# Packed attention, gate and gated MLP on one core: weight folds over four row blocks at once, raw weights in later places, one flat order

## The chip, the core and the metric

The kernel runs on one core of a Trainium2 chip. The time is device microseconds of that core for one execution. Before the change the median of three runs is 605.56 us (605.19 to 606.15).

## The reference, cut to what matters

```
def sm_attn(qq, kk, vv):                                  # float32, scale = 1/8
    s = scale * qq @ kk^T; s = s - max(s)
    a = exp(s); a = a / (sum(a) + 1e-9)
    return a @ vv
p_packed = sm_attn(p, k, v)                               # p: 8 batches, 8 heads, 32 packed queries, 64
x = sm_attn(q, p_packed, p_packed)                        # q, k, v: 8, 8, 576, 64 -> x: 8, 576, 512
gate = sigmoid(causal depthwise convolution of x, 5 taps) # conv_w 5, 512
x = (gate * (x @ w_val)) @ w_out                          # both 512, 512
h = relu(x @ w_in); u, v = h[..., :512], h[..., 512:]     # w_in 512, 1024
v_n = (v - mean(v)) / sqrt(var(v) + 1e-6)
v_s = w_spatial @ v_n + b_spatial                         # over the 576 positions
out = (u * v_s) @ w_out2                                  # 512, 512
```

The weights of the two later parts arrive as float64 words. The kernel makes float32 of them on the chip.

## The kernel before, in words

**Layout.** Channels lie on the 128 partitions, in four blocks, and the 576 positions on the free axis. Large products are made in three passes of split numbers: a value is cut into a high part, which ScalarE casts, and a remainder, which VectorE subtracts (`split`, L134 to 137), and `mm3` (L143) multiplies high by high, high by remainder and remainder by high. All of PSUM is one pool, `ps2`, of four tiles of two banks each.

**Weights.** A raw block is 128 rows of 512 float64 words. `load_raw` (L553) loads it, and `from_f64` (L536 to 547) turns it into float32: ScalarE reads both halves of each word in two passes (L539, L544), VectorE shifts and adds (L545, L547). One such conversion is a unit. Since nothing stands between the gated values and `w_in` but the product with `w_out`, the kernel multiplies these two weights once, in `fold` (L571 to 582), and keeps the product, split, in `wp`. `fold(m, hf)` makes row block m of one half of the columns: four matmuls of 128x512 over k = 0 to 3, in one PSUM tile, then the high part on ScalarE (L580) and the remainder on VectorE (L582). The half of `w_in` that gives v is `winv` (`fv`, hf = 1), the other `winu` (`fu`, hf = 0). The raw blocks lie two by two in the places of later tiles: `w_out` in `wo20` and `ws1`, the v half in `wo21` and `vn1`, `w_val` in `wo20` and `wo21` after those, the u half in `ws1` and `wo20`; the converted u half goes into `wo21`. `spatial` (L584) loads and splits `w_spatial`, `final` (L605) does so with `w_out2`.

**Attention of one batch.** `sa` (L186) makes the scores of the packed queries against k in two PSUM tiles, their maximum and exponential; `tr` transposes; `av` (L228) multiplies by v and divides by the sum, which ends p_packed (`pp`); `ppt` (L258) transposes it. `sb` (L265) makes the scores of q, also in two PSUM tiles, `sn` (L277) their softmax up to the exponential, `sb2` (L292) the sum, the division and a transpose, and then the split into `Ah` and `Al`. `m` (L310) multiplies p_packed by `w_val` to `Mh` and `Ml` (M in what follows), so that `val` (L386) needs only A times M. `xt` (L326) makes x itself, `cv` (L364) the convolution of one channel block in one ScalarE step and four VectorE taps, and the gate from it. For the first batch `cx` makes the gate on TensorE instead, in two halves of 80 matmuls, with tap weights that `cw`, `cb` and a part of `av` prepare.

**MLP of one batch.** `val` makes gate times value, split, for one channel block. `hv` makes one of five position blocks of v, its relu and its normalisation; `hu` one channel block of u; `sp` the spatial product times u, split; `out` one block of the output, which it stores. All of `val`, `hv`, `hu`, `sp` and `out` issue their matmuls at L141.

**What sets the order.** Each piece is a generator, and `run` (L691) walks a written order: a token such as `0hv2.3` takes the generator `hv(2)` of batch 0 three steps further. Tokens without a batch digit are setup pieces or the attention of the first batch; with the digit b, a piece of the attention belongs to batch b + 1. Every engine gets its instructions in just this order and waits in it. SP issues all loads and stores, in order as well. HEAD holds the setup and batches 0 to 2, STEP one batch of the middle (used three times), LAST the end. Loads are tokens too: `ro`, `rw`, `rv` and `ru` raw blocks, `ik`, `ip`, `iv` and `ic` the first k, p, v and conv_w, and `lk`, `lv`, `lp` and `lq` the later ones (k and q share three places, v has two). The name `fv1` repeated four times is thus one fold, step by step.

Of the kernel before, what the change touches and what calls it, by code (L numbers as in the profile page):

```python
# [25 lines left out]
m0 0uu2 cx0 fv0 0uu2 m0.2 0uu2 fv0 cx0 0val2.2 0uu1 0val3 0val2 0val0 0uu1 0val2 0val3 0val2 0val0 0uu1 0val3 0val1
0val0 0val3 0sa0 0val0 0val3 0uu3 0lq0.2 0val1 0val0 1lp0.2 0lq1.2 0uu3 0val1 0uu3 0fu3.3 0sa0 0val1 0fu0 0wo0 0fu3
0fu0 0fu3 0fu0 0fu3 0sa0 0fu0 0val1 0hv0 0wo0 0fu0 0tr0.2 0wo1 0sa0 0wo0 0fu0 0hv4 0tr1.2 0hv0.2 0hv1 0hv4 0hv0 0wo1
0hv4 0hv0 0hv4 0wo1 0hv0 0av0 0hv4 0wo3 0wo1 0hv2 0lv0.2 0av0 0hv4 0hv0 0av0 0wo1 0hv4 0hv1 0hv4 0hv1 0fu2 0wo3 0hv4.2
0fu2 0hv1 0wo3 0hv2 0fu2.2 0hv2 0lk0.2 0wo3 0hv3 0fu2 0hv1 0hv2 0wo3 0fu2 0hv1 0hv2 0hv1 0hv2 0av1 0hv2 0hv3 0fu1 0hv3  # L30
0lv1.2 0fu1 0av1 0hv3 0av1 0fu1 0hv3.2 0ppt0 0fu1 0hv3 0ppt0 0m0 0ws4 0wo1 0fu1 0wo3 0ws4 0sb0.2 0ws0 0fu1 0ws3 0ws0
0hu0 0m0 0lk1.2 0sn1 0wo2 0wo0 0ws4 0hu0 0ws1 0m0 0sn1 0hu1 0hu0 0ws4.2 0sb21 0hu1 0ws2 0wo2 0hu2 0hu1 0ws2 0sb21
0ws4.2 0hu3 0wo2 0hu3 0ws1 1lq0.2 0wo2 0sb21 0hu2 0hu3 0wo2 0ws3 0sp3 0hu2 0wo0 0sn0 0sp2 0wo2 0sn0 0sp2 0sb20 0sp1
0sp2 0sb20 0sp1 0sp2 0sb20 0sp2 0sp0 0sp1.3 0sp0 0xt0 0sp0 0sp3 0sp0 0xt0.2 0sp0 0xt1 0sp3.2 0xt1.2 0sp3 0out3 0cv1
0out2 0cv2 0cv1 0cv0 0out2 0cv3 0out0 0out2 0cv3 0cv1 0out2 1val1 0out0 0cv2 0cv3 1val3 0out0 1val1 0out0 1val3 0out3
# [15 lines left out]
3lq1.2 3val3 3hv0 4lp0.2 3lk1.2 3sa0 3hv1 3hv0.2 3sa0 3hv3 3hv0.2 3hv1 3tr0.2 3sa0 3hv1 3hv2 3hv0 3tr1.2 3hv1 3hv0
3hv1 3hv3 3hv1 3hv3 3av1 3av0 3hv1 3hv3 3lv0.2 3av1 3hu1 3hv2 3lv1.2 3av0 3av1 3hv2 3av0 3hv4 3hv3 3hv2 3hv3 3hv2 3hv3
3hv2 3hu1 3hv4 3hv2 3hv4 3hu2 3hv4 3hu1 3hv4 3hu3 3hv4.3 3ppt0 3hu3 3ppt0 3hv4.2 3sb0.2 3hu3 3sp1 3sn1 3lk0.2 4lq0.2
3sp3 3sn0 3sn1 3sp1 3sb21 3sn0 3hu0 3hu2 3sp1 3sb21 3sb20 3hu0 3hu2 3sp1 3sp2 3hu0 3sp1 3sb20 3sb21 3sp0 3sb20 3sp0
# [723 lines left out]
```

## Time and profile before

| what | value |
|---|---|
| median of three runs | 605.56 us |
| the profiled execution | 605.75 us, its span 603.9 us |
| TensorE busy | 575.3 us, 5267 matmuls |
| VectorE busy | 448.3 us |
| ScalarE busy | 300.3 us |
| DMA, mean over the span | 87 GB/s, 52.55 MB |

The page's second part cuts the span into 40 slices of 15 us. Each digit is the busy share of a slice in tenths (9 is 90% or more); the line DMA is the mean share of the 16 DMA engines:

```profile
PE   1499999999999999999999999999999999999997
DVE  3677879689668988588687987698778978597330
DMA  8990344013220252013220232012311200020002
```

The span is the time from the first to the last instruction that the profiler saw; the measured time also holds 1.85 us around it. A busy time counts only instructions that compute, and the ends of matmuls are modelled. The mean over the span hides that the start and the end look unlike the middle.

### The profile page before, as it was taken

The page shows a single profiled execution, that of the slowest core. Times are in us where ns is not written, and L with a number is a line of the kernel's source. Part 1 is how long each engine was busy: PE and PEld are TensorE (multiplying, and loading weights), DVE is VectorE, ACT ScalarE, POOL GpSimd, SP SyncE. Part 2 cuts the span into 40 slices and gives each one's busy share as a digit, 9 for nine tenths or more (in the row PEclk, how much of TensorE's full clock was granted, in tenths as well). Part 3 has the DMA queues.
Part 4 walks back from the last instruction along what each step waited for, and adds up shares of the span by engine and source line. Part 5 has one row for each costly group of instructions (what it writes and reads, how often), then busy time and mean ns, then how long its engine had stood idle before and what let it go on. Part 6 is the DMA issues. An engine that isn't in the chain of part 4 may idle for free.

```text
span 603.9 us, 12467 instructions
## 1 busy us (share of the span) xinstructions
PE 575.3 (95%) x5267; PEld 504.7 (84%) x5267; DVE 448.3 (74%) x847; ACT 300.3 (50%) x524; POOL 31.2 (5%) x51
## 2 busy tenths in 40 slices
PE   1499999999999999999999999999999999999997
...
DVE  3677879689668988588687987698778978597330
...
DMA  8990344013220252013220232012311200020002
...
DMA packets 16615, 52.55 MB, mean 87 GB/s; under 512 B 1968, under 2 KB 2992, under 8 KB 16560
## 3 DMA queue, kind: packets, MB, share of 16 engines
...
q14 instruction: 14, 0.11, 0.1%
...
## 4 chain that ended last, share of the span: by engine, by line
PE 82%; DVE 9%; DMA 5%; ACT 3%; issue 1%; SPq 0%; DVEq 0%
PE ps L141 71%; PE ps L577 4%; DVE acc L371 4%; DMA kq<-qT 2%; DMA raw<-w_in 2%; PE ps L269 2%; PE ps L234 2%; PE ps L191 1%; DVE g L137 1%; PE ps L332 1%; DMA raw<-w_outT 1%; DVE g L501 1%; PE ps L316 1%; ACT g L135 1%; ACT x L340 1%
## 5 line engine op out<-in xcount | busy, mean ns | idle before, releaser
L141 PEld LDWEIGHTS ps<-ws,vn 128*128 128x128 f32 (+1 forms) x896 | 119.6, 188 | 3.6 <-ACT u L480 1.9
L141 PE MATMUL ps<-ws,vn 128*128 128x288 f32 (+1 forms) x896 | 122.3, 296 | 0.0
L141 PE MATMUL ps<-g,wo 128*128 128x288 f32 x768 | 107.1, 296 | 1.4 <-ACT g L135 0.8
L141 PE MATMUL ps<-g,wp 128*128 128x288 f32 x768 | 107.7, 297 | 0.0
L141 PEld LDWEIGHTS ps<-g,wo 128*128 128x128 f32 x768 | 103.1, 188 | 4.9 <-ACT x L340 2.2
L141 PEld LDWEIGHTS ps<-g,wp 128*128 128x128 f32 x768 | 104.3, 188 | 2.6 <-DVE wp L582 0.5
L371 DVE SCALAR_TENSOR_TENSOR acc<-x,cw,acc 128x572 f32<-128x572 f32 (+1 forms) x112 | 90.1, 815 | 7.6 <-ACT acc L367 4.6
L141 PE MATMUL ps<-wp,g 128*128 128x512 f32 x384 | 94.0, 400 | 1.0 <-DVE g L137 1.0
L141 PEld LDWEIGHTS ps<-wp,g 128*128 128x128 f32 x384 | 71.0, 188 | 20.3 <-issue 2.1
L135 ACT CAST g<-g 128x576 fp32r<-128x576 f32 x64 | 42.8, 674 | 71.4 <-DVE g L501 53.0
L137 DVE TENSOR_TENSOR g<-g,g 128x576 fp32r<-128x576 f32 x64 | 48.2, 753 | 22.9 <-ACT g L135 22.2
L448 POOL TENSOR_TENSOR rstd<-rstd,mhalf 128x1 f32<-128x1 f32 (+1 forms) x40 | 27.3, 683 | 514.0 <-DVE rstd L446 506.6
L501 DVE TENSOR_TENSOR g<-ps,u 128x576 f32<-128x576 f32 x32 | 23.9, 748 | 31.8 <-PE ps L141 31.8
L141 PE MATMUL ps<-Ah,Mh 128*128 128x288 f32 x128 | 38.1, 298 | 0.5 <-DVE Ml L137 0.4
L135 ACT CAST vn<-vr 128x512 fp32r<-128x512 f32 (+1 forms) x40 | 25.1, 627 | 26.2 <-DVE vr L450 26.2
L141 PE MATMUL ps<-Ah,Ml 128*128 128x288 f32 x128 | 37.8, 295 | 0.0
L141 PE MATMUL ps<-Al,Mh 128*128 128x288 f32 x128 | 37.8, 295 | 0.0
L442 DVE BATCH_NORM_STATS2 st<-vr 128x6 f32<-128x512 f32 (+1 forms) x40 | 27.5, 686 | 11.7 <-ACT vr L430 7.0
L430 ACT ACTIVATE vr<-ps 128x512 f32<-128x512 f32 x32 | 19.3, 602 | 32.7 <-PE ps L141 22.9
L137 DVE TENSOR_TENSOR vn<-vr,vn 128x512 fp32r<-128x512 f32 (+1 forms) x40 | 27.3, 682 | 7.8 <-ACT vn L135 7.3
L450 DVE TENSOR_SCALAR vr<-vr,mv,rstd 128x512 f32<-128x512 f32 (+1 forms) x40 | 21.7, 541 | 14.2 <-POOL rstd L448 14.0
L377 ACT ACTIVATE gate<-acc 128x576 f32<-128x576 f32 x28 | 19.2, 687 | 25.7 <-DVE acc L371 25.6
...
## 6 DMA issues: line engine op xcount, KB each, us to landing
...
```

The lines of the kernel that those rows point to most:

```text
L135: nc.scalar.copy(out=hi, in_=src)
L137: nc.vector.tensor_tensor(out=lo, in0=src, in1=f32(hi), op=ALU.subtract)
L141: nc.tensor.matmul(out, lhsT=a, rhs=b, start=(i == 0), stop=(i == len(pairs) - 1))
L234: nc.tensor.matmul(ps[NPK * h:NPK * h + NPK, :65], lhsT=aT[:, 9 * (h // 2) + 4 * (h % 2) + t, :], rhs=v[:, h, t, :], start=(t == 0), stop= ...
L371: nc.vector.scalar_tensor_tensor(out=acc[:, sft:], in0=x[:, :S - sft], scalar=cw[:, c, tap:tap + 1], in1=acc[:, sft:], op0=ALU.mult, op1=A ...
L377: nc.scalar.activation(out=gt, in_=acc, func=AF.Sigmoid)
L430: nc.scalar.activation(out=vr, in_=ps, func=AF.Relu)
L442: nc.vector.bn_stats(st[:w], vr[:w])
L448: nc.gpsimd.tensor_tensor(out=rstd[:w], in0=rstd[:w], in1=mhalf[:w], op=ALU.pow)
L450: nc.vector.tensor_scalar(out=vr[:w], in0=vr[:w], scalar1=mv[:w, 0:1], scalar2=rstd[:w], op0=ALU.subtract, op1=ALU.mult,)
L501: nc.vector.tensor_tensor(out=halves(t), in0=ps[:, :, :SH], in1=halves(self.u.pop(c)), op=ALU.mult)
L577: nc.tensor.matmul(ps, lhsT=woT[k][:, cs], rhs=win[k], start=(k == 0), stop=(k == NC - 1))
```

## The change: what it does

One order, `ORDER`, now writes out all eight batches, and `run` takes no first batch. All its pieces stand in a new order.

The folds no longer take four k in a row for one m. Two row blocks share a PSUM tile (`fps`), four are open at once, and the order takes one k for all m when that block of both weights is converted. Both halves together hold four PSUM tiles, which is all of them.

The raw blocks get places of their own: `w_out` where `wp0` comes to lie, the v half where `wp1` does, `w_val` in `Ml`, `Mh` and `wo20`, the u half in `ws1` and `wo21`. The converted u block is written over the first half of its own raw block. `wp` is therefore made only when the first fold has all its passes. Blocks are loaded one by one, and all four kinds use the early temporaries (pool `g`).

`sa`, `sn` and `sb2` have more places where they can stop, so that the order can put other pieces between their steps. `GATE0` is true, so the first gate is made as before. No instruction is added or left out on any engine.

```diff
--- before.py
+++ after.py
-HEAD = """
-cb0 ro0.2 ik0.2 ip0.2 ro1 ik1.2 lk0.2 ro1 ic0.2 uo0 iv1.2 uo0 uo1 iv0.2 uo1 uo0 rw1 uo1 rw1 uo2 rv0 uo2 sa0 rv0 uo2
-sa0 0ws4 uo3 rw0 cw0 rw0 cw0 0ws0 sa0 uo3 cw0 sa0 cb0 lq0.2 tr0.2 uo3 cb0 uw2 tr1.2 cb0 lq1.2 uw2 uw3 0ws1 uw3 uw2 uv0
-0ru0 uv0 uv1 uw3 lp0.2 av1 0lp0.2 cb0 uv1 uv0 uw0 av0 lv0.2 av1 uv1 av0 av1 uw1 av1 0ru1 av0 0ru1 ppt0 av0 uw0 ppt0
...
-STEP = """
-1val0.2 0out1 0out3 0out1 1val0 0out1 0cv1 0cv3 0out3 1val1 0out3 0out2 0out3 0cv2 0cv3 0out2 1val0 0out2 1val0 0cv2
...
+GATE0 = True
+ORDER = """
+ik0 ip0 ik1 ic0 cw0.3 cb0 rw0 uw0 sa0 cb0 ro0 sa0 cb0 uw0 uo0.2 rw1 uw1 iv1 cb0 sa0 uw0 uo0 fv3 fv2 sa0 uw1.2 ro1
+uo1.3 fv0 ru0 fv1 fv2 iv0 cb0 sa0 tr0 av0 tr1 av1 uu0 rw2 av0 lq0 uu0 uw2 av0 av1 uw2 fv1 av1 ppt0 fv3 uw2 lq1 ppt0
+ro2 uu0 ru1 rw3 av0 sb0 fv0 av1 sn1 uo2 lp0 uo2 fu0 sn1 uo2 uu1 sn0 rv2 uu1 sn1 uw3 ro3 sn1 uw3 uu1 sn0 fu1 uw3 ru3
+sn0 fv3 uo3.2 uv2 uu3 ru2 fv1 uv2 sb21 fu2 fv0 uo3 uu2 rv0 uu3 fv2 fu1 sn0 sb21 wo0 sb20 fu3.2 fu2 lk1 rv3 uu3 fv0 uv2
+uv0 uu2 fv2 uu2 sb21 fv1 sb21 sb20 fv1 sb20.2 rv1 fv1 uv1.2 fv3.2 fv0.2 sb21 uv3 fv3 fu0.2 fu3 fu2 fv2.2 fu3.2 fu0 fu3
+wo3 uv1 ws0 fu2 uv3 uv0 sb20 uv3 fu2.2 cx1 uv0 ws3 wo0.2 0lp0 0lq1 sb20 cx1 sb21 fu1 wo0 fu1.2 ws4 m0.2 wo3 m0 cx0 wo3
+0val0 wo3 fu1 ws3 lv1 ws1 cx0 fu0.2 0val0 ws3 ws2.2 ws4 0val3.2 0val1.2 0val0.2 0val3 0val2.2 0val0 ws1 0val1.2
+0val2.2 lk0 0val1 0val3 0val2 0sa0 0val3 0hv0.2 0sa0 0hv0.2 0sa0 0hv1 ws4 wo0 0hv1.2 0hv0 0sa0 0hu0 0tr0 0hv0.2 ws1
+0sa0 0tr1 0hv1 0hv2.2 0hv1.2 0hv2.2 wo3 0hu0 lv0 wo1 0av0.2 wo0 2lp0 0av0 0hv2 0av1.2 wo3 ws2 0hv4 ws0 0hv2.2 wo1 0hv1
+wo1 wo2 0hv3 0hu0 0hv4 0hv3 0av1 0hv4 0hu2 0hv3.2 0hv4.2 0ppt0 0hv4 0ppt0 ws0 0hu2.2 0lq0 0sb0 0sn1 0hv3.2 wo1 0hv4
+0hv3 0hu3.2 0sn0.2 0hu1.2 ws4.3 wo1 0sn0 0hv4.2 0sn0 ws4 0sn1.2 0sb20.2 0hv4 0sn1 0sb20.3 0sp2 0sp1.2 wo2 0hu3 0sb21.3
...
+0sp3.3 0xt1 0cv3 1val0.2 0sp3 0cv1 wo1 0sp3 0lk0 0out2 1val1.2 0out2 0cv0 0cv2 0out2 0cv1 0cv2 0out0 0out2 0out0.2
+0out1 0cv2 0cv0 0out1.2 0cv3 1val2.2 0out3 0cv1 1val1 0out3 0cv0 1val3 1val2 0cv3 1val3 1val2 1val0.3 1val3 1val1.2
+0out1 0lk1 0out3 1val2 1val3 1sa0 1val3 1hv2.2 1sa0.3 1tr0 1hv1.2 1hu3.2 1lq1 1hv0 1sa0 1hv1 1tr1 1hv2 1av1 1hv1 1av1
...
+6sp1.2 6m0 6sp1 6sn1 6sb21.2 6sp1 6sb21.2 6sp0.2 6sp2 6sb20 6xt0.2 6sp2 6sb21 6sb20 6sp0 6sb21 6sp0 5out2 6sp0 6xt1.2
+6cv1 6sp2 6sp1 6cv1 6sp3 6sp2 6sp3.3 7val2 6sp2 6cv2 6sp3 6cv0 7val0.2 7val2 6cv3 6out1.4 6cv1 6cv2.2 6out3.3 7val1.2
+6out2 6cv0.2 7val0 6out2 7val2 7val1 6cv3 6out0.2 7val0.2 7val1 6cv3 7val2 7val1 7val3.3 6out0 7val2 7val3.2 7hv3
+6out0 7hv3.4 7hv0 7hv3.2 7hv0.2 7hv1.4 7hv4 7hv1.3 7hv0 7hv4 7hu3.2 7hv4.7 7hv0 7hv2 7hu2 7hu3 7hv0 7hv4 7hv2 7hu2.2
+7hu1 7hv2 7hu1.2 7hv2.3 7hu0.3 7hv2 7hv0 7sp0.2 7sp2.2 7sp1 7sp2 7sp3 7sp0.3 7sp2.2 6out2 7sp1.2 7sp3.2 7sp1.2 7sp3.2
+6out2 6out3 7out1 7out0.3 7out2 7out1.3 7out3.4 7out0 7out2.3
 """
@@ -120,8 +124,7 @@
     ps2 = ctx.enter_context(tc.tile_pool(name="ps2", bufs=4, space=bass.MemoryType.PSUM))
 
     wval = const.tile([P, NC, DM], F32)
-    wp = [const.tile([P, NC, 2 * DM], F32R, name=f"wp{i}") for i in range(2)]
-    wo2, ws = [], []
+    wp, wo2, ws = [], [], []
     cw = const.tile([P, NC, CONV], F32)
     ident = const.tile([P, P], F32)
 
@@ -203,6 +206,7 @@
             m4 = sm_p.tile([NPK, 4, 8], F32, tag="m4", name="m4")
...
                 nc.vector.tensor_copy(m4[:, qt, :], mx[NPK * qt:NPK * qt + NPK])
+            yield
             m1 = sm_p.tile([NPK, 8], F32, tag="m1", name="m1")
...
...
-            if self.b == 0:
+            if self.b == 0 and GATE0:
...
@@ -280,8 +284,10 @@
             sTf = sT.rearrange("p a b -> p (a b)")
             for n in range(2):
                 nc.vector.transpose(out=sTf[:, n * SH:(n + 1) * SH], in_=ps[:, n, :SH])
+            yield
             mx = sm_p.tile([P, NB], F32, tag="mx2", name="mx2")
             nc.vector.tensor_reduce(mx, sT, axis=AX.X, op=ALU.max)
+            yield
             nc.vector.tensor_tensor(
                 out=sT, in0=sT, in1=mx.unsqueeze(2).to_broadcast([P, NB, NPK]), op=ALU.subtract
             )
@@ -293,11 +299,14 @@
             sT = self.sT.pop(g)
             sm = sm_p.tile([P, NB], F32, tag="sm2", name="sm2")
             nc.vector.tensor_reduce(sm, sT, axis=AX.X, op=ALU.add)
+            yield
             nc.vector.tensor_scalar_add(sm, sm, 1e-9)
             nc.vector.reciprocal(sm, sm)
+            yield
             nc.vector.tensor_tensor(
                 out=sT, in0=sT, in1=sm.unsqueeze(2).to_broadcast([P, NB, NPK]), op=ALU.mult
             )
+            yield
             an = an_p.tile([P, S], F32, tag="an", name="an")
             nc.vector.transpose(out=an, in_=sT.rearrange("p a b -> p (a b)"))
             self.an[g] = an
@@ -546,36 +555,55 @@
         yield
         nc.vector.tensor_tensor(out=dst, in0=dst, in1=t, op=ALU.add)
 
-    woT, winv, winu = [], [], []
     raws = {}
     early, late = (g_p, "g"), (cv_p, "cv")
-
-    def load_raw(name, slot, w, lo):
-        k0 = int(name[-1]) * 2
-        raw = (vn_p if slot == "vn1" else const).tile([P, 2, 512, 2], I32, tag=slot, name="raw")
-        for i in range(2):
-            if i:
-                yield
-            nc.sync.dma_start(out=raw[:, i], in_=words(w[:, k0 + i, lo:lo + DM]))
-            raws[name[:-1], k0 + i] = raw[:, i]
-
-    def unit(kind, k, dst, temps):
-        return from_f64(dst, raws.pop((kind, k)), DM, *temps)
-
-    def u_half(k):
-        if not winu:
-            t = const.tile([P, NC, DM], F32, tag="wo21", name="winu")
-            winu[:] = [t[:, k, :] for k in range(NC)]
-        return winu[k]
+    blocks = {}
+
+    def block(tag, k, n):
+        if tag not in blocks:
+            blocks[tag] = const.tile([P, n, 2 * DM], I32, tag=tag, name="raw")
+        return blocks[tag][:, k % n]
+
+    def one(tag):
+        return am_p.tile([P, 2 * DM], I32, tag=tag, name="raw", bufs=1)
+
+    places = {
+        "o": lambda k: block("wp0", k, NC),
+        "w": lambda k: block("wp1", k, NC),
+        "v": lambda k: block("wo20", k, 2) if k > 1 else one("Mh" if k else "Ml"),
+        "u": lambda k: block("wo21" if k > 1 else "ws1", k, 2),
+    }
+    homes = {
+        "o": lambda k: woT[:, k],
+        "w": lambda k: winv[:, k],
+        "v": lambda k: wval[:, k],
+        "u": lambda k: raws["u", k].bitcast(F32)[:, :DM],
+    }
+
+    def load_raw(kind, k, w, lo):
+        raw = raws[kind, k] = places[kind](k)
+        nc.sync.dma_start(out=raw.rearrange("p (n t) -> p n t", t=2), in_=words(w[:, k, lo:lo + DM]))
+        yield
+
+    def unit(kind, k):
+        raw = raws[kind, k].rearrange("p (n t) -> p n t", t=2)
+        return from_f64(lambda: homes[kind](k), raw, DM, *early)
+
+    fps = {}
 
     def fold(m, hf):
-        ps = ps2.tile([P, 2, 512], F32, tag="ps2", name="ps2")[:, 0, :]
-        win = winv if hf else winu
+        if (hf, m // 2) not in fps:
+            fps[hf, m // 2] = ps2.tile([P, 2, 512], F32, tag="ps2", name="ps2")
+        ps = fps[hf, m // 2][:, m % 2]
         cs = slice(P * m, P * m + P)
         hs = slice(hf * DM, (hf + 1) * DM)
         for k in range(NC):
-            nc.tensor.matmul(ps, lhsT=woT[k][:, cs], rhs=win[k], start=(k == 0), stop=(k == NC - 1))
-            yield
+            nc.tensor.matmul(
+                ps, lhsT=woT[:, k, cs], rhs=homes["uw"[hf]](k), start=(k == 0), stop=(k == NC - 1)
+            )
+            yield
+        if not wp:
+            wp[:] = [const.tile([P, NC, 2 * DM], F32R, tag=f"wp{i}", name=f"wp{i}") for i in range(2)]
         hi, lo = wp[0][:, m, hs], wp[1][:, m, hs]
         nc.scalar.copy(out=hi, in_=ps)
         yield
@@ -654,14 +682,14 @@
     setup = {
         "cw": lambda i: from_f64(lambda: cw.rearrange("p a b -> p (a b)"), cw64, NC * CONV, *early),
         "cb": lambda i: tap_rows(),
-        "ro": lambda i: load_raw(f"o{i}", ("wo20", "ws1")[i], w_outT, 0),
-        "rw": lambda i: load_raw(f"w{i}", ("wo21", "vn1")[i], w_in, DM),
-        "rv": lambda i: load_raw(f"v{i}", ("wo20", "wo21")[i], w_val, 0),
-        "ru": lambda i: load_raw(f"u{i}", ("ws1", "wo20")[i], w_in, 0),
-        "uo": lambda k: unit("o", k, lambda: woT[k], early),
-        "uw": lambda k: unit("w", k, lambda: winv[k], early),
-        "uv": lambda k: unit("v", k, lambda: wval[:, k, :], early),
-        "uu": lambda k: unit("u", k, lambda: u_half(k), late),
+        "ro": lambda k: load_raw("o", k, w_outT, 0),
+        "rw": lambda k: load_raw("w", k, w_in, DM),
+        "rv": lambda k: load_raw("v", k, w_val, 0),
+        "ru": lambda k: load_raw("u", k, w_in, 0),
+        "uo": lambda k: unit("o", k),
+        "uw": lambda k: unit("w", k),
+        "uv": lambda k: unit("v", k),
+        "uu": lambda k: unit("u", k),
         "fv": lambda m: fold(m, 1),
         "fu": lambda m: fold(m, 0),
         "ws": spatial,
@@ -688,11 +716,11 @@
             return getattr(mls[b], name)(i)
         return getattr(ats[b + 1], name)(i) if b + 1 < B else ()
 
-    def run(order, first):
+    def run(order):
         for tok in order.split():
             tok, _, n = tok.partition(".")
             name = tok.lstrip("01234567")
-            b = -1 if len(name) == len(tok) else first + int(tok[0])
+            b = -1 if len(name) == len(tok) else int(tok[0])
             key = b, name
             if key not in live:
                 live[key] = iter(steps(b, name[:-1], int(name[-1])))
@@ -701,15 +729,10 @@
 
     make_identity(nc, ident)
     nc.vector.memset(mhalf, -0.5)
-    t = const.tile([P, NC, DM], F32, tag="ws0", name="woT")
-    woT[:] = [t[:, k, :] for k in range(NC)]
-    t = vn_p.tile([P, NC, DM], F32, tag="vn0", name="winv")
-    winv[:] = [t[:, k, :] for k in range(NC)]
+    woT = const.tile([P, NC, DM], F32, tag="ws0", name="woT")
+    winv = vn_p.tile([P, NC, DM], F32, tag="vn0", name="winv")
     with tc.manual_schedule():
-        run(HEAD, 0)
-        for b in range(3, 6):
-            run(STEP, b)
-        run(LAST, 6)
+        run(ORDER)
```

## Rows read from the trace of the kernel before

**Rows 1.** The page, part 1: busy us (share of the span) and instructions.
```profile
PE 575.3 (95%) x5267; PEld 504.7 (84%) x5267; DVE 448.3 (74%) x847; ACT 300.3 (50%) x524; POOL 31.2 (5%) x51
```

**Rows 2.** Stretches of the start: busy us (instructions) of each engine, clock, DMA share, GB/s.
```profile
0.00:10.00 10.00, 1.22 (x32) 0.74 (x32) 2.12 (x6) 4.41 (x7) 2.08 (x8) 1.00 0.80 289
10.00:20.00 10.00, 3.18 (x40) 2.39 (x41) 7.04 (x20) 5.99 (x17) 0.00 (x0) 1.00 1.02 416
20.00:30.00 10.00, 4.79 (x94) 3.14 (x92) 6.63 (x16) 6.93 (x14) 1.76 (x3) 1.00 1.03 404
30.00:40.00 10.00, 8.94 (x43) 3.58 (x40) 7.29 (x14) 2.52 (x4) 0.00 (x0) 1.00 1.03 410
```

**Rows 3.** Stretches again, the fold's instructions (L577) alone.
```profile
8.00:55.00 47.00, 14.87 (x32) 6.04 (x32) 1.00 0.79 314
55.00:92.00 37.00, 14.44 (x32) 5.86 (x32) 1.00 0.35 115
```

**Rows 4.** Timeline of TensorE: start us, us, line, operation, count, idle before.
```profile
8.17 1.22 PE L191 MATMUL ps<-kq,pbd 64*32 64x144 f32 x32 [8.17 <-DMA pbd<-pT]
...
32.30 1.03 PE L577 MATMUL ps<-winv,woT 128*128 128x512 f32 x1
...
35.52 9.71 PE L577 MATMUL ps<-winv,woT 128*128 128x512 f32 x22 [0.90 <-DVE winv L547]
...
46.02 2.68 PE L351 MATMUL ps<-an,ppk 32*64 32x288 f32 x80
...
54.65 0.40 PE L141 MATMUL ps<-Ah,Mh 128*128 128x288 f32 x1 [0.42 <-DVE Ml L137]
...
60.41 1.27 PE L191 MATMUL ps<-kq,pbd 64*32 64x144 f32 x64
...
76.94 0.78 PE L234 MATMUL ps<-v,aT 128*32 128x65 f32 x40
...
91.33 1.09 PE L316 MATMUL ps<-wval,ppT 64*32 64x512 f32 x16
92.21 1.18 PE L269 MATMUL ps<-kq,ppT 64*32 64x288 f32 x32
```

**Rows 5.** Timeline of ScalarE: the conversion that waited for w_out's last block.
```profile
13.61 0.66 ACT L539 ACTIVATE tmp<-raw 128x512 f32<-128x512 f32 x1 [3.08 <-DMA raw<-w_outT]
```

**Rows 6.** Groups by line and form: count, busy us, mean ns, idle before.
```profile
L282 DVE STREAM_TRANSPOSE sT<-ps 128x288 f32<-128x288 f32 x32 | 13.5, 460 | 11.6 <-PE ps L269 11.6
...
L284 DVE TENSOR_REDUCE mx<-sT 128x18 f32<-128x576 f32 x16 | 12.0, 753 | 0.5
...
L137 DVE TENSOR_TENSOR Ml<-ps,Mh 128x1024 fp32r<-128x1024 f32 x8 | 9.8, 1223 | 2.3 <-ACT Mh L135 2.3
...
L135 ACT CAST Mh<-ps 128x1024 fp32r<-128x1024 f32 x8 | 8.2, 1028 | 1.4 <-PE ps L316 1.4
...
L582 DVE TENSOR_TENSOR wp<-ps,wp 128x512 fp32r<-128x512 f32 x8 | 5.5, 681 | 0.5 <-ACT wp L580 0.4
...
L210 DVE TENSOR_SCALAR nb<-m 32x8 f32<-32x8 f32 x32 | 5.2, 161 | 0.6
...
L547 DVE CUSTOM_DVE_ANT_0 woT<-woT,tmp 128x1024 uint16<-128x1024 uint16 x4 | 2.6, 678 | 0.1
...
L545 DVE TENSOR_SCALAR woT<-tmp 128x512 int32<-128x512 int32 x4 | 1.7, 425 | 7.1 <-ACT tmp L539 7.1
```

**Rows 7.** Timeline of the tail, VectorE's taps and TensorE.
```profile
534.21 6.65 DVE L371 SCALAR_TENSOR_TENSOR acc<-x,cw,acc 128x572 f32<-128x572 f32 x8
...
545.60 10.29 PE L141 MATMUL ps<-wp,g 128*128 128x512 f32 x43 [0.98 <-DVE g L137]
...
587.62 0.40 PE L141 MATMUL ps<-g,wo 128*128 128x288 f32 x1 [0.84 <-ACT g L135]
...
588.42 11.68 PE L141 MATMUL ps<-g,wo 128*128 128x288 f32 x86 [0.40 <-DVE g L137]
```

More of the change, by code (lines that the diff above doesn't have):

```diff
@@ L26 @@
[L26 to L35, printed above, removed]
@@ L51 @@
[L51 to L54, printed above, removed]
-3sp2 3sp0.3 3sp3 3sp2.2 3xt0 3sp2 3m0 3sp3 3xt0.2 3xt1 3sp3 3m0 3sp3 3out0 3xt1.2 3m0 3out0 3cv0 3cv1 3cv0 3out1 3cv2
@@ new lines @@
+1sn0 1sb20 1sn1.3 1sb21.3 0out0 1sb21 1hu2 1sb20.2 1sp3.2 1lv0 1sb21.2 1sp3.2 1sp2 1sp0.2 1sp3 1sb20.2 1sp1.3 1sb20
+1xt0.2 1sp1 1lk1 1sp2 0out3 1sp2.2 1sp0 1xt1.2 1cv0 2val0 1sp1 2val0 1cv3 1sp2 1out2.2 1cv0 1out2.2 1cv2 1cv3 1lv1
+1out0 1out1.2 1cv0 1cv1 1out3 1out0 1cv3 1out1 1out3.2 1cv1 2val0 2val1.2 2val2 1cv2 1cv1 2val1 1lp0 2val2 2val0.2
+2val3.2 1cv2 2val2 2val1 1lk0 2val1 1out0.2 2sa0 2val3 2val2.2 2val3 2lq1 2val3 2hv0 2hv3 2hv0 2sa0.2 2hu1.2 2sa0
+2hv0.2 2tr0 2sa0 2tr1 2hv3 2hu1 2hv0.2 2hv3 2hv0 2hu0 2hv2 2hv3.2 2av1.2 2hv3 2av0 2hv3 2hv2.3 2av1 2lv1 2av0.2 2hv1
@@ new lines @@
+2ppt0 2hv1.2 2ppt0 2hv1 2hu0 2sb0 2hv2 2sn0 2hv4 2hv2.2 2sn1 2hv4.3 2sn0 2hv1.2 2sn1 2hv4.3 2hu0 2hu2.2 2hv4 2sn1 2hv1
+2hu2 2hu3.3 2hv4.2 2sp1.2 2sn0.2 2sp1 2sb20 1out1 2sp0.2 2sb20 2sp1 2lv0 2sb20.2 2sp1 2sn1 2sb21.2 2sp2.2 1out3
+2sb21.3 2lk1 2sp0.3 2sb20.2 2sp2.2 2lk0 2sp3.3 2sp2 2xt0.2 2sp3.2 2m0.2 2xt1 2sb21 2xt1 2cv0 2m0 2out1 2cv3 2out1 2cv0
+2out1 3val2 2cv2 2cv3 2out2 2out0 2cv1 2out2 3val0.2 2out1 2out2.2 2cv1 3val1 2cv2 2cv0 3val0 3lq1 2out0.2 3val2 2cv3
+3val1 2cv1 3val1 2out3 2cv2 2out3 3val2 3val3.2 3val0.2 3val1 3sa0 3val3 3val1 3val2.2 3val3 2out3 3lq0 3val3 3hv0.2
```

57 lines of the change are left out of this document (25 added, 32 removed).

## The prediction

> **What bounds the kernel now.** I read the engine shares first, then the first 40 us slice by slice, then the order of TensorE's work there, and the tail last. TensorE is busy 575.3 of 603.9 us [rows 1], so 28.6 us are idle. The slices show where: busy 1.22, 3.18, 4.79 and 8.94 us of each 10 [rows 2] leaves 21.9 us idle before 40 us. In the tail an idle 0.98, 0.84 and 0.40 us stand in front of three runs of matmuls, and the last run ends at 588.42 + 11.68 = 600.1 [rows 7], 3.8 us before the end. That leaves 0.7 us for all batches between. Only the start can give much.
>
> In the start the transfers run flat out: DMA share 1.02 and 1.03 at 404 to 416 GB/s [rows 2]. TensorE has little to do because the fold (w_out times w_in) needs converted blocks of two weights, and a row block takes its four k in turn: its first pass is at 32.30, the long run at 35.52 [rows 4]. The V half's 32 passes stand ahead of 55 us, the U half's 32 behind it [rows 3], in time in which TensorE does nothing but work. The first matmul of `val` is at 54.65 [rows 4].
>
> **The change part by part.** Every engine issues the same instructions; no transfer is added. Order, places and waits change.
>
> *Transfers.* A raw block is 128 x 512 float64, 512 KB, 1.28 us at 410 GB/s. In the old order the eighth transfer (the last of four w_out blocks, three k and p: 3840 KB, 3.93 MB) was there at 13.6 [rows 5]; 3.93 MB are 9.6 us, so a landing is 4.0 us plus the bytes up to it. New order: both k and p, 1216 KB, at 7.0; the first pair (w_in's V block 0, w_out's block 0), 2260 KB with conv_w's 20, at 9.6; q, 6760 KB with both v (650 each), at 20.9; the last w_val block, 13032 KB, at 36.5. Each raw block lies in a place that nothing used before, so SP waits for none of the 16. It does wait at `0lq1`, until ScalarE has converted w_out2's block 0, with four loads and `lk0` behind it; `0sa0`, the next that needs them, comes some 10 us later, so I cost it at nothing; uncovered it would be some 4 us.
>
> *First fold.* Scores at 7.0 + 1.22 [rows 4] = 8.2. VectorE then has two 576-wide passes of 0.75, nine small of 0.16, two shifts of 0.42 and two adds of 0.68 [rows 6]: 5.1 us, with hops 13.7. From there TensorE folds k = 0 for all four m: four blocks, eight passes.
>
> *Clock.* The granted column prints 1.00 from the start [rows 2], but 32 score matmuls took 1.22 us at 8.17 and 64 took 1.27 us at 60.41 [rows 4]: at the start the array ran at its half level, 1.2 GHz. One fold pass still took 1.03 us at 32.30; 22 passes from 35.52 took 9.71, 0.43 each, at 2.4 GHz [rows 4]. It rose in between, when scores and folds had run almost without pause. So in the new order a pass costs 0.86 or 0.43. I take four of the first eight at the half level: 5.2 us, to 18.9. Ends: none of them (-1.7 us), and all 14 passes before the second scores (6.0 instead of 1.7: +4.3).
>
> The Trainium skill ("TensorE: Matmul & The Clock Gate", "Part 1: The HAM clock gate") says that the throttled state is the default and that activity releases it, which speaks against folding in short bursts between waits. By that page the fold would run at the half level until its bursts join, the +4.3 end. The doubled durations agree with it; the printed column does not.
>
> *To the second scores.* One block of k = 1 (0.86) to 19.8, `av` twice at 0.78, two more blocks of k = 1 around the small chain to ppT, and `sb` 1.18 [rows 4]: 24.5.
>
> *VectorE to M.* From there VectorE has no gap in the new order, and M waits for it. Ten units are left, 10 shifts x 0.425 + 10 adds x 0.68 = 11.0; `sn` twice (two transposes of 0.46, two passes of 0.75) 4.8; `sb2` twice (three passes of 0.75, two small) 5.4; six fold remainders x 0.68 = 4.1: 25.3 us in 44 instructions [rows 6]. Eight taps took 6.65 [rows 7], 0.02 between two beyond their 0.81: another 0.9. From 24.7 to 51.0. The last w_val block's first step is reached at about 44, seven us after its landing; u's in-place shift, which now also waits for ScalarE's second pass, comes to the front later than that pass. Then `m` 1.09 [rows 4], its copy 1.03 and its remainder 1.22 [rows 6], with hops: `val` at 54.9, 0.25 later than now.
>
> *TensorE meanwhile.* 24.5 + 46 passes x 0.43 = 44.3. The first gate half needs PSUM that the fold holds until VectorE's fourth remainder, at 46.6 by the same sums; 2.68 [rows 4] for it and four last passes end at 51.0, as VectorE does. The second gate half, another 2.68, fills the time in which `m` becomes M. So by `val` all 64 passes are done instead of 32: 32 x 0.43 = **13.8 us** leave the part in which TensorE is the bound. But there is no room: a further wait shows at once.
>
> *What is late next.* Behind M's remainder VectorE has a w_out2 unit (1.1), two fold remainders (1.4), one of w_spatial (0.75), and the gated values' four products, four remainders and three small casts before the first `hv` can end: 9.7 us, at 65.1 with hops. TensorE is there after 48 passes x 0.134, `sa` 1.27 and nine passes x 0.235 [rows 4, 7], at 64.7, and VectorE stays full until the first `sp`. I take **-0.8** (0 to -2).
>
> *Batches 1 to 6.* In the new order four `cv` stand ahead of the gated values on VectorE: 16 taps x 0.83 + ten passes x 0.75 + 2.5 before = 23.3 us, against 22.5 us of TensorE work (`val`, `out`, `sa`, nine passes of `hv`). At worst 0.8 for each of six; I take **-1.0** in all (0 to -5).
>
> *Tail.* Before the last `hv` an `out` (3.2 us) now stands between `val`s and covers the 0.98. Before the last `out` the halves of `sp1` and `sp3` alternate, so one remainder is made while the other's matmuls run; of the idle 1.24 half is left. **+1.5** (0 to +2.2).
>
> Sum: 13.8 - 0.25 - 0.8 - 1.0 + 1.5 = 13.2 us. The profiled execution took 605.75, 0.19 above the median shown; 605.75 - 13.2 = 592.5, by the median 592.4.
>
> **Rivals.**
>
> 1. *All goes well*: full clock at the first fold (1.7), no loss in the batches (1.0) nor at `hv` (0.8), the tail's whole 2.2: 13.2 + 1.7 + 1.0 + 0.8 + 0.7 = 17.4, 588. For it: 0.7 us of loss in today's batches. Against: VectorE's sum has no slack.
>
> 2. *The clock stays at the half level up to the second scores*: `val` 4.3 us later, `av` and `sb` 1 us: 13.2 - 5.3 = 7.9, 598. For it: half level at 8.17 and still at 32.30 [rows 4]. Against: it was up within a few passes of the first folds.
>
> 3. *The fold's four PSUM tiles hold up the head.* They are all of PSUM; gate halves, `m` and `val` wait in a row for copies on ScalarE and VectorE. Two such waits of 4 us beyond my sums: 600.5. If M comes 13 us later than now, nothing is won, and the change does not do what its order says.
>
> 4. *Slower.* VectorE's four `cv` ahead of the gated values delay the first `hv` of every batch. It decides from 13.2 / 7 = 1.9 us a batch; my sums give 0.8 at worst. At 2.1 a batch: 607. A k load that SP holds behind a store (`0out1` ahead of `0lk1`) would come at the same place. Against it: today's batches have the same passes before `hv` and lose 0.7 us in all.
>
> **How the numbers follow.** Forecast (589 to 596.5) 0.56; rival 1 0.13; rival 2 0.13; rival 3 0.11, of it 0.03 near no change; rival 4 0.07. The unknown costs reach from 4.2 us better to 9.5 worse than the sum; with a tenth left out at either side the range is 587 to 600. A difference under 0.2% (1.2 us) can't be told from none. Faster 0.90, same 0.03, slower 0.07.
>
> **What would show it.** Right: fold passes from about 13.7 and all 64 ahead of the first `val` matmul, that one at 54 to 56; TensorE's idle time in the first 40 us well under 21.9; VectorE almost without gaps from 25 to 52; shorter idle pieces in the tail. Wrong at the clock: fold passes of 0.86 us beyond 20. Wrong at PSUM: TensorE idle for several us between 45 and 55, ended by fold remainders. Wrong in the batches: over 1 us idle before each first `hv`. The forecast falls if `val` starts after 60.

## The result: 587.87 us instead of 605.79

The changed kernel takes 587.87 us (median of four runs, 587.46 to 588.5), the kernel before 605.79 in the same comparison (605.19 to 606.15). The ratio is 0.9706 (0.9689 to 0.9723), so 17.9 us went. The forecast was 592.5 with 587 to 600 as its range, so the time lies at the lower edge of it; rival 1 had said 588. The profiled execution took 587.61 us, its span is 585.8.

The page of the changed kernel, part 1, answers to [rows 1]: TensorE does the same 5267 matmuls, in 5.1 us less of busy time, and is idle for 15.6 us instead of 28.6.

```profile
PE 570.2 (97%) x5267; PEld 503.1 (86%) x5267; DVE 442.8 (76%) x847; ACT 298.1 (51%) x524; POOL 27.3 (5%) x51
```

The stretches of its start, with the columns of [rows 2]: TensorE is idle for 8.9 of the first 40 us (21.9 before), while the DMA share is the same up to 30 us. So the loads are no faster; there is work beside them.

```profile
0.00:10.00 10.00, 2.84 (x66) 1.64 (x66) 1.51 (x5) 2.65 (x6) 3.64 (x11) 1.00 0.79 270
10.00:20.00 10.00, 8.33 (x19) 4.70 (x20) 7.35 (x20) 8.51 (x19) 0.00 (x0) 1.00 1.03 419
20.00:30.00 10.00, 9.96 (x129) 4.26 (x128) 7.71 (x20) 4.74 (x10) 0.00 (x0) 1.00 1.03 406
30.00:40.00 10.00, 10.00 (x25) 4.43 (x24) 9.43 (x19) 7.84 (x15) 0.00 (x0) 1.00 0.92 360
```

The fold's instructions alone (L601 now), as in [rows 3]: all 64 records lie ahead of the first `val`, none behind it.

```profile
8.00:56.00 48.00, 31.40 (x64) 12.45 (x64) 1.00 0.77 299
56.00:92.00 36.00, 0.00 (x0) 0.00 (x0) 1.00 0.40 139
```

TensorE's timeline, columns as in [rows 4]. The first ten fold records take 0.68 us each, later ones 0.43: from start to start the first five step by 0.85 us or more, the others by 0.43. The column of the granted clock prints 1.00 above all the same, but the trace has no clock record ahead of 18.5 us, which is where the steps shorten. At 46.67 TensorE has waited 1.85 us. `val` starts at 55.86, 1.2 us later than before, with 32 more fold records done; `hv` follows the scores at 63.60 without a wait. In the last `out`, 0.99 us remain of the tail's three pauses in [rows 7].

```profile
14.04 6.75 PE L601 MATMUL ps<-winv,woT 128*128 128x512 f32 x10 [1.67 <-DVE woT L556]
...
24.27 1.20 PE L273 MATMUL ps<-kq,ppT 64*32 64x288 f32 x32
...
36.07 3.60 PE L601 MATMUL ps<-winv,woT 128*128 128x512 f32 x8
...
46.67 1.12 PE L601 MATMUL ps<-raw,woT 128*128 128x512 f32 x2 [1.85 <-DVE wp L610]
47.72 2.68 PE L360 MATMUL ps<-an,ppk 32*64 32x288 f32 x80
50.34 1.98 PE L601 MATMUL ps<-raw,woT 128*128 128x512 f32 x4
52.25 1.09 PE L325 MATMUL ps<-wval,ppT 64*32 64x512 f32 x16
53.27 2.67 PE L360 MATMUL ps<-an,ppk 32*64 32x288 f32 x80
55.86 0.40 PE L144 MATMUL ps<-Ah,Mh 128*128 128x288 f32 x1
...
63.60 5.74 PE L144 MATMUL ps<-wp,g 128*128 128x512 f32 x24
...
569.40 12.50 PE L144 MATMUL ps<-g,wo 128*128 128x288 f32 x92 [0.99 <-DVE g L140]
```

The waits of TensorE over the whole span (who waited for whom: us in total, times, longest): only the 1.0 at the end lies behind `val`. No batch waits for VectorE ahead of its `hv`.

```profile
PE ps L194 <- DMA pbd<-pT: 4.9, 1, 4.9
PE ps L601 <- DVE wp L610: 1.8, 1, 1.8
PE ps L601 <- DVE woT L556: 1.7, 1, 1.7
PE ps L194 <- DMA kq<-kT: 1.5, 1, 1.5
PE ps L144 <- DVE g L140: 1.0, 1, 1.0
PE ps L668 <- ACT cwt L664: 0.8, 1, 0.8
```

**Where the 18.1 us of the two profiled executions went.** TensorE's lost time at a point is the start of the matmul there less the sum, over all matmuls before it, of the step that their kind takes in undisturbed runs (0.429 us a fold record, 0.133 for 288 columns, 0.233 for 512, and so on for the small kinds). All steps together are 562.4 us in either kernel. (Other steps for the small kinds would move both columns of lost time alike, and the gains stay.)

| up to | lost before | lost after | gained in this part | forecast |
|---|---|---|---|---|
| first `val` | 28.31 | 15.80 | 12.5 | 13.55 |
| first `hv` | 28.24 | 16.00 | -0.3 | -0.8 |
| first `hv` of the last batch | 34.37 | 18.19 | 3.9 | -1.0 |
| end of the span | 41.5 | 23.4 | 1.9 | 1.5 |
| sum | | | 18.1 | 13.2 |

The head and the tail came out near their terms. The batches came out 4.9 us better, and they are the whole surprise.

### The profile page after: what moved, and what is told of

It reads as the page before. It is cut to its first block, busy times and chain, and to the rows that moved or that the text cites. A ratio compares the mean times of both kernels' runs of the same rounds, so it can differ in the third digit from the quotient of the medians.

```text
span 585.8 us, 12443 instructions
## 1 busy us (share of the span) xinstructions
PE 570.2 (97%) x5267; PEld 503.1 (86%) x5267; DVE 442.8 (76%) x847; ACT 298.1 (51%) x524; POOL 27.3 (5%) x51
## 4 chain that ended last, share of the span: by engine, by line
PE 93%; DVE 4%; DMA 1%; ACT 1%; issue 0%; SPq 0%; DVEq 0%; ACTq 0%
PE ps L144 82%; PE ps L601 2%; PE ps L238 2%; PE ps L194 2%; PE ps L341 2%; PE ps L273 2%; PE ps L325 1%; DMA kq<-kT 1%; PE ps L360 1%; DVE wp L610 1%; DVE sT L286 0%; DVE sT L306 0%; DVE mx L202 0%; DVE sm L301 0%; DVE raw L556 0%
## 5 line engine op out<-in xcount | busy, mean ns | idle before, releaser
L144 PE MATMUL ps<-g,wo 128*128 128x288 f32 x768 | 105.9, 295 | 1.0 <-DVE g L140 1.0
L144 PE MATMUL ps<-wp,g 128*128 128x512 f32 x384 | 91.9, 393 | 0.0
L457 POOL TENSOR_TENSOR rstd<-rstd,mhalf 128x1 f32<-128x1 f32 (+1 forms) x40 | 23.6, 593 | 522.2 <-DVE rstd L455 447.6
L535 ACT COPY o<-ps 128x576 f32<-128x576 f32 x32 | 20.3, 635 | 35.7 <-PE ps L144 35.7
L439 ACT ACTIVATE vr<-ps 128x512 f32<-128x512 f32 x32 | 19.2, 602 | 34.9 <-PE ps L144 32.3
```

Of the source, the lines that this page charges most:

```text
L144: nc.tensor.matmul(out, lhsT=a, rhs=b, start=(i == 0), stop=(i == len(pairs) - 1))
L439: nc.scalar.activation(out=vr, in_=ps, func=AF.Relu)
L457: nc.gpsimd.tensor_tensor(out=rstd[:w], in0=rstd[:w], in1=mhalf[:w], op=ALU.pow)
L535: nc.scalar.copy(out=halves(t), in_=ps[:, :, :SH])
```

## The experiments

In the batches one thing stands out in the groups by line and form (count, busy us, mean ns of one): `hv`'s 384 matmuls of 512 columns have become faster, although they are the same instructions. First the kernel before, then the changed one.

```profile
L141 PE MATMUL ps<-wp,g 128*128 128x512 f32 x384 | 94.0, 400 | 1.0 <-DVE g L137 1.0
```

```profile
L144 PE MATMUL ps<-wp,g 128*128 128x512 f32 x384 | 91.9, 393 | 0.0
```

From one start to the next, which is called a step here, the median is 234 ns before (232 to 235 by batch) and 227 after, in every batch. The order of the work differs, and so do the places of the two `wp` tiles in SBUF: `wp0` and `wp1` began at bytes 9344 and 25728 of each partition, now at 38048 and 21664. `g`, the other operand, begins at 155808 in both.

**e1: the changed kernel with wp moved back to multiples of 64 bytes.** The pad ahead of `wp1` moves both `wp` tiles by 32 bytes, the second pad lies behind them, so that `g` moves by 64.

```diff
         if tag not in blocks:
+            if tag in ("wp1", "ws1"):
+                const.tile([P, 8], F32, name=f"pad_{tag}")
```

> The changed kernel with two pads of 32 bytes, so that both wp tiles begin 32 bytes later, on multiples of 64 bytes as they did before the change; nothing else on any engine changes. Theory (the place of wp sets the pace of hv's 384 matmuls of 512 columns): a step from one to the next goes from 227 back to about 234 ns, 384 x 7 ns = 2.7 us, so about 590.5 us. Rival (the new order gave the pace): steps stay at 227 ns and the time at 587.9 us.

Measured: 589.44 us, ratio 0.9744 (0.9732 to 0.9757) against 0.9706 of the changed kernel, so 2.3 us of 605 lost. The group of e1:

```profile
L144 PE MATMUL ps<-wp,g 128*128 128x512 f32 x384 | 94.4, 399 | 0.2 <-DVE g L410 0.2
```

The step is 234 ns again. So a shift of 32 bytes undoes it; the order has no part in the pace.

**e2: the kernel before with wp 32 bytes later.** The same pads around its `wp` (8 floats ahead, 8 behind; `g` moves by 64).

> The kernel before with wp 32 bytes later and nothing else changed. Theory (the place sets hv's pace): hv's steps go from 232 to 235 ns to 227 ns, some 2.5 us less, about 603.2 us. Rival (order): no change, 605.7 us.

Measured: 604.68 us, ratio 0.9996 (0.9987 to 1.0005), group 94.1 us. The theory falls in this form: a start that is no multiple of 64 is not what counts. What differed from the changed kernel was the distance to `g`.

**e5: the kernel before, wp 32 and all behind it 128 bytes later** (8 floats ahead, 24 behind).

> The kernel before with wp 32 bytes later and everything behind it, g among it, 128 bytes later, so that wp and g (the two operands of hv's matmuls) begin at the same place within 128 bytes, as in the changed kernel; in the kernel before they were 32 apart, in e1 and e2 too (32 and 64). Theory (hv's pace hangs on how wp and g lie to each other): hv's steps at 227 ns instead of 234, 384 x 7 ns = 2.7 us less, about 602.6 us. Rival (another property of the changed kernel, such as which of the two wp tiles lies lower): 234 ns, no change, about 605 us.

Measured: 604.26 us, ratio 0.9991 (0.9982 to 1.0), group 93.7 us. The same place within 128 bytes is not enough.

**e6: the changed kernel, wp, g and what lies between 32 bytes later** (8 floats ahead of `wp1`).

> The changed kernel with wp, g and everything between 32 bytes later, so that wp and g lie to each other as before. Theory (their relative place): hv's steps stay at 227 ns and the time at 587.9 us. Rival (the absolute place of wp, as e1 would also have it): 234 ns and some 590.4 us.

Measured: 587.75 us, ratio 0.9715 (0.9702 to 0.9728), group 91.9 us, step 227. A shift of both by 32 bytes changes nothing: the distance is kept, and so is the pace.

**e9: the kernel before with wp 32 bytes later and `g` where it was.** (Two small tiles behind `wp`, `cw` and `ident`, move with it.) Then `g` begins 143 x 1024 bytes behind `wp0`; in the changed kernel and in e6 it is 115 x 1024. In the kernel before and in e1 the distance was 32 bytes off a multiple of 256, in e2 64, in e5 128.

```diff
+    mhalf = const.tile([P, 1], F32)
     wp = [const.tile([P, NC, 2 * DM], F32R, name=f"wp{i}") for i in range(2)]
...
-    mhalf = const.tile([P, 1], F32)
```

> The kernel before with one constant of 32 bytes allocated ahead of wp instead of behind it, so that wp alone lies 32 bytes later; g, vn and the spatial and output weights stay where they were. wp and g are then whole multiples of 1024 bytes apart, as in the changed kernel and in e6; in e5 they were 128 bytes off such a multiple, in e1 32, in e2 64. Theory (the distance of hv's two operands sets its pace): 227 ns a step instead of 234, some 2.7 us less, about 602.4 us. Rival (something else of the changed kernel, such as the lower place of the second wp tile): 232 to 234 ns, at most 0.8 us less.

Measured: 603.15 us, ratio 0.9965 (0.9952 to 0.9977): 2.1 us gained by moving one constant of 32 bytes. The step is 227 ns again (228 in one batch). The groups of e2, e5, e6 and e9:

```profile
L143 PE MATMUL ps<-wp,g 128*128 128x512 f32 x384 | 94.1, 400 | 1.0 <-DVE g L139 1.0
```

```profile
L143 PE MATMUL ps<-wp,g 128*128 128x512 f32 x384 | 93.7, 399 | 1.0 <-DVE g L139 1.0
```

```profile
L144 PE MATMUL ps<-wp,g 128*128 128x512 f32 x384 | 91.9, 393 | 0.0
```

```profile
L142 PE MATMUL ps<-wp,g 128*128 128x512 f32 x384 | 92.0, 395 | 1.0 <-DVE g L138 1.0
```

So in seven layouts the group takes 91.9 to 92.0 us at the three with an exact distance and 93.7 to 94.4 at the four without. Lost time from the first `hv` to that of the last batch goes from 6.13 (before) to 4.18 (e9), and from 2.19 (after) to 4.73 (e1): the place is worth 2.0 to 2.5 of the 3.9 us. The other 1.4 to 2.0 are left to the new order, and the traces say where: from the first `hv` to that of the third batch e9 loses 2.1 us more than the changed kernel, from there to that of the last batch 0.1 less. So the new order gains in the first two batches, and nothing in the five behind them; which of its moves does it was not tried.

**e3: the fold's four k in turn again.** Of each fold the tokens of k = 0 to 2 were moved to just ahead of that of k = 3.

> The changed kernel with each fold's passes of k = 0, 1 and 2 moved to just ahead of its pass of k = 3, so that nothing is folded before the last blocks are converted; loads, places and all other pieces stay. Theory (the gain is fold work that runs while the loads still come in): TensorE starts folding at about 34.6 us, then has 64 records x 0.43 = 27.5 us, both first gate parts and M before val: val at about 68.5 us instead of 55.9, and 587.9 + 12.6 = 600.5 us. Rival (places and the order of the loads gave most of it): val within 3 us of 55.9, at most 591 us.

Measured: 598.19 us, ratio 0.9886 (0.9872 to 0.99), 10.9 us of 605 lost. TensorE of e3:

```profile
26.33 1.12 PE L600 MATMUL ps<-winv,woT 128*128 128x512 f32 x2 [0.39 <-DVE woT L555]
32.86 13.94 PE L600 MATMUL ps<-winv,woT 128*128 128x512 f32 x26 [5.41 <-DVE woT L555]
46.64 10.46 PE L600 MATMUL ps<-raw,woT 128*128 128x512 f32 x24
57.03 2.68 PE L359 MATMUL ps<-an,ppk 32*64 32x288 f32 x80
```

`val` starts at 66.9 instead of 55.86, with the same work done. The new order and places alone, the pace of `hv` among them, bring 7 us of the 18; folding as blocks land brings the rest. (`val` came 1.6 us sooner than expected: six records ran before 32.86 and the long run began 1.7 us sooner, less what the half level cost.) The 26 records from 32.86 take 0.54 us each: the granted clock of 32.80:40.00 is 0.64, after 5.41 us without a matmul. Some 2.6 us of the loss (26 x 0.53 instead of 26 x 0.43) are thus the half level.

```profile
27.00:32.80 5.80, 0.46 (x2) 0.00 (x0) 5.80 (x12) 4.76 (x9) 0.00 (x0) 0.86 1.03 410
32.80:40.00 7.20, 7.14 (x11) 3.13 (x12) 6.60 (x15) 2.05 (x4) 0.00 (x0) 0.64 0.85 328
```

**e4: one pass ahead of a copy in the same tile.** In the order, `fu3.2 fu0 fu3 wo3 uv1 ws0 fu2` became:

```diff
-fu3.2 fu0 fu3 wo3 uv1 ws0 fu2
+fu3 fu2 fu3 fu0 fu3 wo3 uv1 ws0
```

> The changed kernel with one pass moved: the last k of the u half's row block 2 goes ahead of the copy of row block 3, which lies in the same PSUM tile. Theory (TensorE's 1.85 us without work at 44.8 us are a wait for that copy's remainder, because the two row blocks share a tile): the pass runs at about 44.9 us, the first gate part can start when the v half's last remainder is done, at about 46.1 instead of 47.7, and val comes up to 1.6 us sooner: 586.3 to 587 us. Rival (VectorE sets val, through Al and M): no change, 587.9 us.

Measured: 587.09 us, ratio 0.9696 (0.9682 to 0.971). `val` came at 55.12, 0.7 us sooner. TensorE of e4:

```profile
24.91 1.20 PE L273 MATMUL ps<-kq,ppT 64*32 64x288 f32 x32
...
40.14 6.17 PE L601 MATMUL ps<-raw,woT 128*128 128x512 f32 x14
46.24 3.12 PE L360 MATMUL ps<-an,ppk 32*64 32x288 f32 x80
```

The 1.85 us are gone: the pass waited only because its row block shares a PSUM tile with one that was being copied out. The time gain of 0.6 us lies within the intervals, and 0.7 us at `val` is no more than profiles of one order differ by: with the changed kernel's order of the start, `val` comes at 54.89 (e6) to 55.86. What differs there is the time up to the second scores, which took 0.6 us longer in this profile. From the second scores to `val` the changed kernel, e1, e6, e8 and e12 take 31.59 to 31.63 us, e4 takes 30.21. So the moved pass is worth 1.4 us in this stretch. It isn't the whole 1.85, since the first gate part now waits for the next tile within its run (3.12 instead of 2.68).

**e7: twelve extra matmuls in the idle start.**

```diff
+    def warm(ps, n):
+        for _ in range(n):
+            nc.tensor.matmul(ps, lhsT=ident, rhs=ident, start=True, stop=True)
```

> The changed kernel with twelve extra 128x128 matmuls on the identity where TensorE waits in the first 14 us: six ahead of the first scores, two ahead of the tap rows, four ahead of the first fold. They write places that the next matmul overwrites. Theory (the array is at its half level because it idles; the first folds pay for it): the first ten fold records take some 0.43 us each, 4.3 instead of 6.7 us, and the second scores come up to 2 us sooner, val too: 585.5 to 586.5 us. Rival (the level doesn't rise in this time, or VectorE and the loads hold val anyway): 587.9 us, or with the extra matmuls in the way up to 2 us more.

Measured: 587.05 us, ratio 0.9699 (0.9686 to 0.9713), not to be told from the changed kernel. TensorE of e7, and four stretches of it (the eighth value is the granted clock):

```profile
14.08 5.49 PE L609 MATMUL ps<-winv,woT 128*128 128x512 f32 x10
...
45.47 1.12 PE L609 MATMUL ps<-raw,woT 128*128 128x512 f32 x2 [1.88 <-DVE wp L618]
46.53 4.37 PE L366 MATMUL ps<-an,ppk 32*64 32x288 f32 x80
```

```profile
5.00:7.00 2.00, 1.08 (x32) 0.62 (x32) 0.00 (x0) 0.00 (x0) 0.00 (x0) 1.00 0.94 269
...
10.00:12.00 2.00, 2.00 (x10) 1.98 (x10) 1.85 (x10) 1.96 (x4) 0.00 (x0) 0.50 1.02 420
...
16.00:18.00 2.00, 2.00 (x5) 0.88 (x5) 1.71 (x3) 2.00 (x7) 0.00 (x0) 0.96 1.02 415
```

```profile
46.60:51.00 4.40, 4.40 (x81) 2.73 (x82) 4.22 (x8) 3.06 (x5) 0.00 (x0) 0.61 0.36 91
```

The first ten records cost 5.49 us instead of 6.75. The clock record of this trace begins at 5.9 us with the full level (the 32 scores after the wait of 1.47 us for k took 0.72 us, 1.22 in the changed kernel); it falls to half at 9.3 and is back at 16.1. And after the pause of 1.88 us the first gate part ran mostly at 1.2 GHz, 4.37 us instead of 2.68, which took the gain back in this execution, the slowest of five (588.14; the others 586.48 to 587.11, without a profile).

The gain at the first records is no steady one either. Without extra matmuls they took from 6.15 (e6) to 7.34 us (e4), with them 6.56 and 7.37 in e10 and e11 below, where the level also rose early (at 4.8 and 5.5 us), fell again (8.2 and 12.4) and was back at 18.5 and 19.2. In the changed kernel and in e1, e4, e6, e8 and e12 it rose at 16.9 to 19.7. So twelve small matmuls did not lift the level for good in any of the three, and whether idling alone holds it down in the start stays open.

**e8: a block of w_val in an older block's place.** In `places`, block 1 of `w_val` goes to `wo20`, after block 2.

> The changed kernel with w_val's block 1 in the place of its block 2, as raw blocks shared places before: its load, which SP issued at 27.8 us, must now wait for ScalarE's second pass over block 2, at about 34 us, with the later loads behind it. Theory (raw blocks in places of their own are a part of the gain): the block lands some 6 us later, at 44 to 45 us, its unit holds ScalarE and VectorE, and val comes 2 to 5 us later: 590 to 593 us. Rival (that load has slack): 587.9 us.

Measured: 587.18 us, ratio 0.9707 (0.9693 to 0.972): the same. SP of e8 (a row is an issue, with the wait inside it) holds the load back as expected, to 33.70:

```profile
25.98 8.05 SPq L585 DMA_DIRECT2D raw<-w_val  x2
34.12 0.41 SPq L635 DMA_DIRECT2D raw<-w_out  x1
```

It still landed at 37.53, and at 38.20 in the changed kernel, where it queued behind other transfers. So this place is worth nothing; for the other blocks it wasn't tried.

**e10 and e11: the two repairs together, and the copies ahead.** e10 is e4 and e7 in one; e11 also moves `fv3`'s remainder and `fv2`'s copy and remainder ahead of `sb21` and `uv3`.

> e4's moved pass and e7's twelve extra matmuls together in the changed kernel. Theory (each hides the other's gain: in e4 the folds still begin at the half level, in e7 a pause of 1.88 us ahead of the first gate part was followed by that part at the half level, 4.37 instead of 2.68 us): no such pause, first gate part 2.7 us, val at about 53.5 us, 585 to 586 us. Rival (VectorE's remainders hold the first gate part all the same): a pause of over 1 us stays ahead of it and the time at 587 us.

> e10, and the copies and remainders of the v half's row blocks 3 and 2 ahead of other work on ScalarE and VectorE, so that all the fold's first two PSUM tiles are free some 1.2 us sooner. Theory (the four PSUM tiles hold the first gate part): it starts right behind the folds, no pause over 0.3 us between 26 and 55 us, val at about 53 us, 584.5 to 585.5 us. Rival (VectorE is full, and what is put ahead makes Al and M later by as much): as e10.

Measured: e10 586.16 us, ratio 0.9681 (0.9668 to 0.9694); e11 585.82, ratio 0.9683 (0.9669 to 0.9696). TensorE of e10, then of e11:

```profile
14.25 6.56 PE L609 MATMUL ps<-winv,woT 128*128 128x512 f32 x10
...
45.64 3.14 PE L366 MATMUL ps<-an,ppk 32*64 32x288 f32 x80
...
51.64 2.87 PE L366 MATMUL ps<-an,ppk 32*64 32x288 f32 x80
```

```profile
13.50 7.37 PE L609 MATMUL ps<-winv,woT 128*128 128x512 f32 x10 [1.38 <-DVE woT L562]
...
45.70 2.68 PE L366 MATMUL ps<-an,ppk 32*64 32x288 f32 x80
...
51.41 3.24 PE L366 MATMUL ps<-an,ppk 32*64 32x288 f32 x80
```

`val` starts at 54.5 and 54.7 us, not at 53.5 and 53. e10 has no pause ahead of the gate, and its gate parts run at the full level; its first ten folds took 6.56 us all the same. From the second scores to `val` it takes 30.2 us and e11 30.3, as e4 does with the pass alone: the extra matmuls brought nothing here. e11 frees the tiles sooner (the first gate part takes 2.68), and the second gate part then waits instead: it comes out as e10, as its rival said. Both are some 1.4 us under the changed kernel by the ratios, which is what e4's pass is worth, with intervals that touch its own.

**e12: the tail without alternating halves.** `7sp1 7sp2 7sp3` became `7sp1.2 7sp2 7sp3`.

> The changed kernel with the second half of the last batch's sp1 moved ahead of the first half of sp3, so that the halves of the two don't alternate before the last out. Theory of the prediction (alternating lets one remainder be made beside the other's matmuls and is worth some 0.6 us): the pause in the last out is 1.4 to 1.7 us instead of 0.99, 588.4 us. Rival (in either order sp3's product, copy and remainder end last): a pause of 0.7 to 1.1 us, later in the run of matmuls, and 587.9 us.

Measured: 587.12 us, ratio 0.9703 (0.9689 to 0.9718). The last `out` of e12:

```profile
569.20 12.50 PE L144 MATMUL ps<-g,wo 128*128 128x288 f32 x92 [0.99 <-DVE g L140]
```

The pause is the same and comes after the same four matmuls. It was not the halves that shortened it. In both versions `sp1`'s remainder stands behind `sp3`'s product on VectorE. In e12's trace `sp1`'s high part was there at 565.46, VectorE idled until `sp3`'s product at 567.72, and made the remainder behind it, from 568.39 to 569.14; the matmul at 569.20 waited for that. An order with the remainder ahead was not tried.

## Why the prediction held, and which step failed

**Transfers, right within 1.7 us.** The last `w_val` block was forecast at 36.5 and landed at 38.2. It cost nothing: no engine waits for a load between the second scores and `val`.

**First fold, right.** Forecast from 13.7, seen at 14.04. Second scores at 24.5, seen at 24.27.

**Clock, right in kind.** Four records at the half level were taken (1.7 us lost); it was the first five of ten, which took 6.75 us instead of 4.29, some 2.4 us lost. All 14 passes at the half level, the +4.3, did not come.

The Trainium skill ("TensorE: Matmul & The Clock Gate", "Part 1: The HAM clock gate") says that the throttled state is the default and that activity releases it. The trace agrees: the level was at half up to 18.5 us and rose within one unbroken run of ten passes. The prediction had read this as holding until the second scores.

**VectorE to M, 1.2 us short.** From the second scores to `val` 30.4 us were forecast (24.5 to 54.9). It took 31.6, with all 64 records ahead of `val`, and 30.2 with e4's order. So the work on VectorE was sized right (it was busy 24.84 of the 27 us from 25 to 52); what had no term is that one fold pass waits for a remainder of its tile's other row block. From that pass on TensorE has no gap up to `val`, while VectorE, done with `Al` at 51.41, idles 2.53 us ahead of M's remainder: M waited for TensorE's turn, not for VectorE. That is rival 3's mechanism at 1.85 us, not 8.

**What is late next, small.** `hv` was to lose 0.8 us to the gated values, since VectorE would finish them at 65.1. VectorE finished them at 66.01, yet `hv` lost only 0.3: its first matmuls need only the first gated block, there at 61.71, so it started at 63.60 and met the others as they came.

**Batches 1 to 6, wrong.** "I take -1.0 in all" was +3.9. Two things failed in it. The four `cv` ahead of the gated values cost nothing: lost time over these batches is 2.19 us, 0.3 a batch, and rival 4 with its 1.9 a batch is out. And the part on the transfers took the new places as a matter of waits alone; that a new place of `wp` changes the pace of 384 matmuls (e1, e9) had no term. Without these 2.0 to 2.5 us the time would have been about 590, inside the likeliest case's own range. The rest of the +3.9 came in the first two batches (e9).

**Tail, right in size, wrong in cause.** +1.5 was 1.9: the 0.98 is gone, 1.24 became 0.99. Some 0.3 more are the pace of `hv`'s 48 matmuls in the last batch; 0.4 have no cause here. Alternating halves has no part in it (e12).

The head, which was the reason for the forecast, held by its mechanism. That the whole time came out 4.6 us below the forecast and still in the range is in part luck: the batches gained where a loss was forecast, half of it and more by a shift of places that nobody aimed at. Rival 1 named the time, for another reason: its 1.7 us of clock did not come, and its sum had no loss in the batches where there was a gain.
